# One pool of eight PSUM banks, corrected durations and a new order for a planned recurrence-and-attention kernel

## The chip, the cores and the metric

One core of one Trainium2 chip. The metric is the device time of one execution in microseconds: 377.94 us, the median of three runs (376.17 to 379.87). The profiled execution took 377.4 us, of which the span from the first to the last instruction is 375.6 us.

## What is computed

Two stages, for batch 4, 768 positions, 8 heads of width 48 (model width 384). The first is a linear recurrence per head, the second an attention by four experts, two of which are kept per position.

```
for t in range(768):                      # per batch and head; state is 48 x 48
    y[t]  = r[t] @ (state + (u * k[t]) outer v[t])
    state = w[t][:, None] * state + k[t] outer v[t]
x = y, heads side by side                 # 4 x 768 x 384
for e in range(4):                        # q, k, v = x @ wq[e], x @ wk[e], x @ wv[e], width 64
    ye = softmax(causal(q k^T / 8)) v @ wo[e]
    out += (e among the top 2 of x @ w_gate) * gate weight * ye
```

All inputs and the output are float32.

## The kernel before

**Units.** The work is cut into eight units (batch b, half g of the sequence, 384 positions each). A unit has a recurrence part, `rwkv`, and an attention part, `moe`.

The recurrence part treats four pairs of heads, one after the other. A pair loads three tiles (`lt`, `nat`, `vy`). VectorE runs two scans over the decays (`suf` L376, `pre` L380); GpSimd or VectorE multiply keys and queries by them (`kt` L385, `mr` L387). TensorE transposes the scaled keys (`ktp` L415), which are copied to SBUF (`kts`). Three TensorE products follow: `aps` (L431, 24 matmuls of 64x64), masked by VectorE into `am`; `ups` (L445 and L446, 24 matmuls), copied into `ust` and scanned by VectorE into the states `ys` (L453); and `yps` (L475 and L478, 48 matmuls), which reads `am` and `ys` and is added to `xn` by VectorE (L484). After the pairs three transposes `xp` (L498) turn `xn` into `xh` and a rest `xl`, so that later products keep float32 accuracy in three passes.

The attention part projects `xh`, `xl` to queries and keys (`pp` L544) and to values and gate logits (`vp` L567). Then for two pairs of experts and three row blocks come scores (`sp` L632), maximum with mask on VectorE (L638), exponential on ScalarE (L644), transposes of the probabilities (`tp` L657) with their copies, the product with the values (`yp` L680), the gate weights (`gp`, `gb`), and the output projection (`op` L751) with its store.

**Tilings.** TensorE's array is used in four tilings, which the planner calls modes: the whole 128x128 (transposes, projections, `vp`, `op`, `gp`, `gb`, and the filler `warm`), 64x64 for `aps`, `ups`, `yps` (mode "q"), 64x128 for `sp` ("r"), 128x64 for `yp` ("h").

**What sets the order.** Nothing is scheduled by the compiler. `Plan.add` collects every step with a set of engines and their assumed durations, its data dependencies, its buffers, and a wished place in the order: `want`, the progress of its unit (from `T0`, `MV`, `LEAD`) plus an offset by kind (`OFF`, and `OFF0` for the first unit's recurrence). `Plan.order` then simulates all engines and emits the instructions engine by engine. At each step it takes, of those of an engine's first 40 candidates that could start within `SLACK` nanoseconds of the earliest, the one with the lowest `want`; on TensorE a candidate in the tiling that the array already has counts as lower by `STAY`. A change of tiling is charged `DRAIN` (100 ns) plus `ENTER` by kind. A step that needs a buffer is no candidate until one of its tag is free. Once emitted, the order on each engine is fixed; semaphores make it correct whatever the true durations are.

**PSUM.** There are eight banks. `bank(tag, ...)` takes one from the pool of its tag: four for `sc` (scores, always two at a time; one is held by the filler `warm` until its last matmul), two for `mo` (the attention's other products: `pp`, `vp`, `tp`, `yp`, `gp`, `gb`, `op`), two for `rw` (the recurrence: `ktp` 1, `aps` 1, `ups` 2, `yps` 2, `xp` 1). In the last unit `mo` products alternate between `mo` and `rw`. The table `BANK` can send a tag to another pool; it is empty.

**Fillers.** 94 matmuls `warm` on constant data keep TensorE busy: 14 at the start, 80 with the lowest urgency, which go where nothing else can start.

Of the kernel before, what the change touches and what calls it, by code (L numbers as in the profile page):

```python
# [41 lines left out]


def t_exp(cols):
    return 237 + 0.834 * cols


def t_pool(cols):
# [3 lines left out]
class Slot:  # L52
# [6 lines left out]
    def __call__(self):  # L59
        if self.ap is None:  # L60
# [6 lines left out]

WAITS = {"PE": dict(PE=0, DVE=215, ACT=215, POOL=260, SP=200), "DVE": dict(PE=139 + SAFE, DVE=127, ACT=128, POOL=164, SP=130),
         "ACT": dict(PE=164 + SAFE, DVE=143, ACT=127, POOL=170, SP=130), "POOL": dict(PE=150 + SAFE, DVE=140, ACT=150, POOL=128, SP=130),
         "SP": dict(PE=2000, DVE=2000, ACT=2000, POOL=2000, SP=2000)}  # L70

# [137 lines left out]
def rwkv_moe(ctx: ExitStack, tc: tile.TileContext, wkr, vY, nat, uN,  # L209
# [6 lines left out]
    plan = Plan()  # L216
    E_ = {"DVE": nc.vector, "ACT": nc.scalar, "POOL": nc.gpsimd, "SP": nc.sync}

    def sb(shape, dt, tag, name):
        return Slot(wk, shape, dt, tag, name)  # L220

    def bank(tag, name, dt=F32, whole=True):
        return Slot(ps, [128, 2048 // mybir.dt.size(dt)], dt, BANK.get(tag, tag), name, whole)

# [289 lines left out]
    def moe(b, g, v0, v1):  # L514
        xh, xl = XS[b, g]
# [59 lines left out]
        def gates():  # L575

            m1 = sb([128, 3], F32, "m1", f"m1{n0}")
            rank = sb([128, 3, E], F32, "rank", f"rank{n0}")
            c1 = sb([128, 3, E, E], F32, "c1", f"c1{n0}")
            c2 = sb([128, 3, E, E], F32, "c2", f"c2{n0}")  # L580
            lgk = [(lg, i) for i in range(3)]

            V = nc.gpsimd

            def compare(e):
                la = lg()[:, :, None, :].to_broadcast([128, 3, E, E])
# [12 lines left out]
            plan.add("gate", {"POOL": 1440}, ranks, lgk + ["masks", m1], [c1, c2, rank, ge])  # L599
            plan.add("gate", {"ACT": 250}, lambda e: nc.scalar.activation(ge(), ge(), AF.Exp), [ge], [ge])  # L600
            plan.add("gate", {"DVE": 100}, lambda e: nc.vector.scalar_tensor_tensor(
                ge(), rank(), 1.5, ge(), op0=ALU.is_lt, op1=ALU.mult), [rank, ge], [ge])

            def norm(e):
                V.tensor_tensor(c1()[:, :, 0, 0:2], ge()[:, :, 0:2], ge()[:, :, 2:4], op=ALU.add)
                V.tensor_tensor(gs(), c1()[:, :, 0, 0], c1()[:, :, 0, 1], op=ALU.add)
                V.tensor_scalar(gs(), gs(), 1e-9, None, op0=ALU.add)
            plan.add("gate", {"POOL": 875}, norm, [ge, c1], [gs, c1])
# [79 lines left out]
        gg = sb([128, 3, E], F32, "gg", f"gg{n0}")  # L688
        gT = sb([128, 128], BF16, "gT", f"gT{n0}")

        def gather():

            g3 = sb([128, 128], BF16, "g3", f"g3{n0}")
            gp = mbank(f"gp{n0}", BF16)

            def over(e):
                nc.vector.scalar_tensor_tensor(gg(), asum(), 1e-9, gs()[:, :, None].to_broadcast([128, 3, E]),
                                               op0=ALU.add, op1=ALU.mult)
                nc.vector.reciprocal(gg(), gg())
# [12 lines left out]
            plan.add("g4", {"POOL": 1290}, parts, [gg], [gg, g3])  # L712
            plan.add("gp", {"PE": 60}, lambda e: nc.tensor.transpose(
                gp()[:, 0:128], g3(), identb), [g3], [gp])
            plan.add("gT", {"DVE": 131}, lambda e: nc.vector.tensor_copy(gT(), gp()[:, 0:128]), [gp], [gT])
# [42 lines left out]
        yps = []  # L758
# [15 lines left out]
        parts = [weigh(ep, yps[ep]) for ep in range(2)]  # L774
# [28 lines left out]
    for k, u in enumerate(units):  # L803
        spare[0] = k == len(units) - 1
        moe(*u, starts[k], starts[k] + MV[u[1]])
    for o in plan.order(dict(PE=7200.0 - 216 * WARM[0], DVE=3000.0, ACT=1700.0, POOL=3000.0, SP=560.0), SLACK):
        o["fn"](o["e"])


FLEX, LATE, SLACK = (True, True, 118.4)  # L810
BUFS = dict(lt=4, nat=3, ys=2, vy=3, suf=2, pre=3, am=2, kt=2, rk=2, kts=2, xn=2, xh=2, xl=2, lg=2, asum=2, ge=2, m1=2, rank=2, c1=1, c2=1,
            gs=2, mx0=6, mx1=4, a=4, gg=2, gT=2, g3=2, yr=2, yh0=1, yh1=1, yl0=1, yl1=1, ob=2, v_sb0=1, v_sb1=1, ATa=3, ATb=2,
            sc=4, mo=2, rw=2)
BUFS.update({f"{n}{l}{ep}": m for n, m in (("K", 1), ("Q", 2)) for l in "hl" for ep in range(2)})
# [78 lines left out]
```

## Time and profile before

| | |
|---|---|
| median of three runs | 377.94 us |
| the profiled execution | 377.4 us |
| its span | 375.6 us |
| TensorE matmul | 363.2 us, 97% |
| TensorE weight load | 281.4 us, 75% |
| VectorE | 309.2 us, 82% |
| ScalarE | 236.9 us, 63% |
| GpSimd | 144.3 us, 38% |
| granted TensorE clock, mean | 0.994 |

The busy time of an engine is the union of its instructions' durations. Matmuls are pipelined: one lasts longer than the distance to the next. So the time that a matmul costs is read from the start of one to the start of the next in the timeline, and a matmul that starts late shows no idle time while the one before it still counts as running.

### The profile page before, as it was taken

What the parts mean: (1) busy time and instruction counts of PE and PEld (TensorE: products, weight loads), DVE (VectorE), ACT (ScalarE), POOL (GpSimd) and SP (SyncE); (2) the same over time, 40 slices, a digit from 0 to 9 for tenths busy, and PEclk for the clock granted to TensorE, in tenths of its full rate; (3) what the DMA queues carried; (4) which work ended last, traced back from release to release, by engine and by line L of the source; (5) the groups of instructions that cost most, each with busy time, mean ns of one, the idle gap of its engine ahead of it and who ended that gap; (6) DMA issues with size and microseconds to landing.
All of it is one profiled execution on the core that took longest, in us unless ns stands there. A gap on an engine that the chain in (4) does not pass through costs nothing.

```text
span 375.6 us, 12545 instructions
## 1 busy us (share of the span) xinstructions
PE 363.2 (97%) x5046; PEld 281.4 (75%) x5046; DVE 309.2 (82%) x838; ACT 236.9 (63%) x658; POOL 144.3 (38%) x254
## 2 busy tenths in 40 slices
PE   6999999999999999999989999999999999999985
PEld 2555787778867778888876878888886878789653
DVE  6999999999997996999986996999996864467461
ACT  2475465975957767575765766575785754666562
POOL 3246666585651653263331553363431402002000
PEclk9899999999999999999999999999999999999999
DMA  7798454544543444525324343624222001001001
GB/s 231 282 353 268 144 172 132 184 130 137 189 138 128 128 128 122 185 78 191 112 83 126 112 145 92 193 83 135 75 65 65 3 3 65 1 2 63 2 2 65
DMA packets 18059, 45.18 MB, mean 120 GB/s; under 512 B 2000, under 2 KB 9424, under 8 KB 18000
## 3 DMA queue, kind: packets, MB, share of 16 engines
q1 hardware_dynamic: 18000, 44.37, 36.9%
q8 instruction: 40, 0.66, 0.7%
q14 instruction: 19, 0.16, 0.1%
HBM read 39.64 MB, written 4.72 MB: 118 GB/s over the span
## 4 chain that ended last, share of the span: by engine, by line
PE 80%; DVE 11%; DMA 3%; ACT 2%; issue 2%; POOL 1%; SPq 0%; POOLq 0%; DVEq 0%; ACTq 0%
PE pp L544 11%; PE yp L680 10%; PE sp L632 10%; PE tp L657 9%; PE vp L567 7%; PE op L751 6%; PE aps L431 5%; PE yps L475 5%; PE warm L791 4%; PE ups L445 3%; DVE suf L376 2%; PE ktp L415 2%; PE xp L498 2%; PE yps L478 2%; DVE ys L453 2%
## 5 line engine op out<-in xcount | busy, mean ns | idle before, releaser
L644 ACT ACTIVATE a<-a,mx 128x128 f32<-128x128 f32 (+5 forms) x96 | 63.8, 666 | 10.2 <-DVE mx L638 9.5
L657 PE MATMUL tp<-ident,a 128*128 128x128 f32 x336 | 56.6, 284 | 1.6 <-ACT a L644 1.0
L638 DVE CUSTOM_DVE_ANT_0 a<-sp,cmask 128x384 f32<-128x384 f32 (+4 forms) x96 | 44.8, 495 | 14.9 <-PE sp L632 14.2
L657 PEld LDWEIGHTS tp<-ident,a 128*128 128x128 f32 x336 | 37.3, 140 | 12.1 <-ACT a L644 5.5
L392 POOL TENSOR_TENSOR nat<-nat,u_sb 128x288 f32<-128x288 f32 x30 | 29.4, 979 | 37.9 <-PE tp L657 16.7
L227 ACT COPY ATa<-tp 128x512 f32<-128x512 f32 (+3 forms) x68 | 32.8, 487 | 16.5 <-PE tp L657 16.1
L385 POOL TENSOR_TENSOR kt<-lt,suf 128x384 f32<-128x384 f32 x27 | 29.2, 1082 | 23.5 <-DVE suf L376 16.3
L544 PE MATMUL pp<-xh,wh_qk 128*128 128x384 f32 x96 | 38.0, 396 | 0.0
L387 POOL TENSOR_TENSOR pre<-lt,pre 128x384 f32<-128x384 f32 x22 | 22.9, 1040 | 37.5 <-DVE pre L380 21.7
L405 ACT ACTIVATE xn<-nat,rk 128x48 f32<-128x48 f32 x117 | 30.0, 325 | 10.5 <-DVE rk L398 10.0
L680 PE MATMUL yp<-ATa,v_sb 128*64 128x384 f32 (+2 forms) x224 | 36.4, 450 | 0.0
L376 DVE TENSOR_TENSOR_SCAN suf<-lt,one_suf 128x390 f32<-128x390 f32 x32 | 34.3, 1078 | 2.3 <-DMA lt<-in_wkr_dram 2.0
L453 DVE TENSOR_TENSOR_SCAN ys<-ust,wdec 112x384 f32<-112x384 f32 x32 | 33.4, 1046 | 0.9 <-ACT ust L227 0.6
L380 DVE TENSOR_TENSOR_SCAN pre<-lt,inv_pre 128x390 f32<-128x390 f32 x32 | 32.6, 1018 | 0.1
L544 PE MATMUL pp<-xl,wh_qk 128*128 128x384 f32 x96 | 32.3, 337 | 0.0
L544 PE MATMUL pp<-xh,wl_qk 128*128 128x384 f32 x96 | 32.3, 336 | 0.0
L475 PE MATMUL yps<-ys,pre 64*64 64x48 f32 (+1 forms) x768 | 30.9, 262 | 0.1
L383 ACT COPY wdec<-suf 128x288 f32<-128x288 f32 x32 | 22.7, 710 | 12.9 <-DVE suf L376 6.7
L431 PEld LDWEIGHTS aps<-pre,kt 64*64 64x64 f32 x768 | 24.8, 134 | 7.5 <-issue 3.1
L791 PE MATMUL warm<-one_suf 128*128 128x512 bf16 x94 | 28.3, 420 | 1.4 <-POOL one_suf L247 1.4
L431 PE MATMUL aps<-pre,kt 64*64 64x64 f32 x768 | 28.8, 222 | 0.4
L475 PEld LDWEIGHTS yps<-ys,pre 64*64 64x64 f32 (+1 forms) x768 | 21.6, 133 | 9.0 <-issue 2.5
(135 smaller groups left out, 944.3 us busy)
## 6 DMA issues: line engine op xcount, KB each, us to landing
lt<-in_wkr_dram SPq DMA_DIRECT2D x31, 579.5 KB, 4.1
nat<-in_nat_dram SPq DMA_DIRECT2D x32, 432.0 KB, 3.4
vy<-in_vY_dram SPq DMA_DIRECT2D x32, 144.0 KB, 2.2
out_dram<-ob SPq DMA_DIRECT2D x24, 192.0 KB, 1.9
w_qk<-in_wqk_dram SPq DMA_DIRECT2D x1, 768.0 KB, 5.7
w_vg<-in_wvg_dram SPq DMA_DIRECT2D x1, 390.0 KB, 6.2
lt<-in_wkr_dram SPq DMA_DIRECT2D x1, 384.0 KB, 5.1
w_o<-in_wo_dram SPq DMA_DIRECT2D x1, 384.0 KB, 6.7
```

What stands on the lines that cost most here:

```text
L227: nc.scalar.copy(o, i)
L376: plan.add("suf", {"DVE": t_scan(WB)}, lambda e, suf=suf, w_=w_: nc.vector.tensor_tensor_scan(rev(suf()), rev(w_()), rev(one_suf), 0.0, op ...
L431: nc.tensor.matmul(a_[half(h), c * C:(c + 1) * C], k[half(h), c, :], m[half(h), c, 0:C], start=True, stop=True)
L453: plan.add("ys", {"DVE": t_scan(D * NX)}, lambda e, ys=ys, us=us, wd=wd: nc.vector.tensor_tensor_scan(flat(ys()[0:112]), flat(us[0:112]), ...
L475: nc.tensor.matmul(yps[h]()[half(q), o], pre()[r, c, 0:C], ys()[r, :, c], start=i == 0, stop=False)
L544: nc.tensor.matmul(pp()[:, 0:384], w[:, qk, k, cs], x()[:, k, :], start=(k == j == 0), stop=(k == j == 2))
L632: nc.tensor.matmul(sps[x]()[:, 0:w], q()[p, t], flat(k())[p, o], start=j == 0, stop=j == 2)
L638: plan.add("max", {"DVE": t_dve(w) + T_RED}, lambda e, x=x, a=a, mx=mx, h=h, o=o, m=m, sps=sps: nc.vector.tensor_tensor_reduce(a()[:, o], ...
L644: plan.add("exp", {"ACT": t_exp(n)}, lambda e, x=x, y=y, mx=mx, a=a: nc.scalar.activation(a()[:, 0:n], a()[:, 0:n], AF.Exp, bias=mx[-1](), ...
L657: nc.tensor.transpose(tp()[:, j * 128:(j + 1) * 128], a()[:, (j0 + j) * 128:(j0 + j + 1) * 128], ident)
L680: nc.tensor.matmul(yp()[e * 64:e * 64 + 64, lo:384], v_sb[ep]()[:, j, e * 64:e * 64 + 64], at, start=(j == 0), stop=(j == nj - 1))
L791: plan.add("warm", {"PE": 216}, lambda e: nc.tensor.matmul(w()[:, 0:512], wz[:, 0:128], wz, start=True, stop=True), [], [w], want=1e6 if i ...
```

## The change

The instructions, their data and their shapes stay. Three things change. First, `BANK` sends the tags `rw` and `sc` to `mo`, whose pool now has all eight banks, so any product may take any free bank. Second, the planner's assumptions: an exponential costs 40 ns more, a maximum 12 ns more, the GpSimd steps `gate` (L599) and `g4` (L712) 190 and 1160 ns more; a load counts as landed 2700 ns after its issue instead of 2000, and small loads cost 200 ns more; VectorE is free at 3800 ns instead of 3000, the load queue at 740 instead of 560. Third, the order is another: every offset in `OFF` and `OFF0`, the pacing `MV`, `LEAD`, `T0`, `T1`, the `SLACK`, and `STAY`, which goes from 3.04 to 12.46.

```diff
 def t_exp(cols):
-    return 237 + 0.834 * cols
+    return 277 + 0.834 * cols
...
-         "SP": dict(PE=2000, DVE=2000, ACT=2000, POOL=2000, SP=2000)}
+         "SP": dict(PE=2700, DVE=2700, ACT=2700, POOL=2700, SP=2000)}
...
-        plan.add(kind, {"SP": max(475.0 if cols > 0 else 650.0, abs(cols) * 512 / 360.0)},
+        plan.add(kind, {"SP": max(475.0 if cols > 0 else 650.0, abs(cols) * 512 / 390.0 + (200.0 if abs(cols) < 400 else 0.0))},
...
-            plan.add("gate", {"POOL": 1440}, ranks, lgk + ["masks", m1], [c1, c2, rank, ge])
+            plan.add("gate", {"POOL": 1630}, ranks, lgk + ["masks", m1], [c1, c2, rank, ge])
...
-            plan.add("g4", {"POOL": 1290}, parts, [gg], [gg, g3])
+            plan.add("g4", {"POOL": 2450}, parts, [gg], [gg, g3])
...
-    for o in plan.order(dict(PE=7200.0 - 216 * WARM[0], DVE=3000.0, ACT=1700.0, POOL=3000.0, SP=560.0), SLACK):
+    for o in plan.order(dict(PE=7200.0 - 216 * WARM[0], DVE=3800.0, ACT=1700.0, POOL=3000.0, SP=740.0), SLACK):
         o["fn"](o["e"])
...
-FLEX, LATE, SLACK = (True, True, 118.4)
+FLEX, LATE, SLACK = (True, True, 126.8)
...
-            sc=4, mo=2, rw=2)
+            mo=8)
...
-BANK = {}
+BANK = {'rw': 'mo', 'sc': 'mo'}
...
-T_RED = 0
+T_RED = 12
...
-MV = {0: 29.57, 1: 45.97}
-LEAD = (-8.87, -3.98)
+MV = {0: 25.79, 1: 54.18}
+LEAD = (-2.91, -8.85)
...
-STAY = 3.04
+STAY = 12.46
...
-T0, T1 = (30.81, 25.29)
+T0, T1 = (28.53, 22.07)
```

## Rows read from the trace of the kernel before

**Rows 1.** The page's first two parts: busy time of each engine with its share of the span, and the granted TensorE clock in 40 equal slices (tenths of full speed).

```profile
PE 363.2 (97%) x5046; PEld 281.4 (75%) x5046; DVE 309.2 (82%) x838; ACT 236.9 (63%) x658; POOL 144.3 (38%) x254
...
PEclk9899999999999999999999999999999999999999
```

**Rows 2.** The view by stretches: from and to in us, length, then busy us and number of instructions of PE, PEld, DVE, ACT and POOL, the granted clock, the DMA share and GB/s.

```profile
0.00:40.00 40.00, 35.80 (x514) 20.51 (x515) 34.90 (x74) 18.73 (x48) 18.86 (x30) 0.96 0.81 281
40.00:362.00 322.00, 318.05 (x4480) 255.21 (x4479) 270.83 (x757) 214.50 (x604) 124.62 (x221) 1.00 0.33 104
137.60:223.36 85.76, 83.97 (x1240) 67.81 (x1239) 75.28 (x207) 56.84 (x158) 34.14 (x60) 1.00 0.41 127
```

**Rows 3.** The timeline of TensorE (start, length, line, operation, tiles, number merged): the first and the last stay in a tiling between 40 and 362 us, and the two places where the same stretch of one batch begins anew.

```profile
40.57 0.91 PE L431 MATMUL aps<-pre,kt 64*64 64x64 f32 x24
...
137.60 0.88 PE L498 MATMUL xp<-ident,xn 128*128 128x128 f32 x6
...
223.36 0.87 PE L498 MATMUL xp<-ident,xn 128*128 128x128 f32 x6
...
362.65 2.03 PE L680 MATMUL yp<-ATa,v_sb 128*64 128x384 f32 x8
```

**Rows 4.** The same timeline at places that show the price of a change of tiling: one projection step alone between two `ups`, one `aps` alone, and two `aps` on end, each with what starts next.

```profile
42.96 0.44 PE L544 MATMUL pp<-xh,wh_qk 128*128 128x384 f32 x1
43.24 0.33 PE L544 MATMUL pp<-xh,wl_qk 128*128 128x384 f32 x1
43.41 0.34 PE L544 MATMUL pp<-xl,wh_qk 128*128 128x384 f32 x1
43.71 0.25 PE L445 MATMUL ups<-nat,kts 64*64 64x48 f32 x1
...
163.95 0.91 PE L431 MATMUL aps<-pre,kt 64*64 64x64 f32 x24
164.79 0.44 PE L544 MATMUL pp<-xh,wh_qk 128*128 128x384 f32 x1
...
168.25 1.61 PE L431 MATMUL aps<-pre,kt 64*64 64x64 f32 x48
169.80 0.34 PE L724 MATMUL gb<-gT,sel 128*128 128x128 bf16 x3
```

**Rows 5.** The view of single lines: all TensorE instructions of a line with their number, duration in ns (least, median, most), and first and last start.

```profile
L431 PE MATMUL aps<-pre,kt x768: 217/218/268, 12.9 to 317.2; 64*64 64x64 f32 x192
...
L445 PE MATMUL ups<-nat,kts x384: 218/218/339, 11.0 to 315.7; 64*64 64x48 f32 x192
...
L475 PE MATMUL yps<-ys,pre x768: 244/266/279, 14.9 to 318.8; 64*64 64x48 f32 x183, 48*64 48x48 f32 x9
...
L632 PE MATMUL sp<-Kh,Qh x128: 301/409/502, 53.1 to 357.7; 64*128 64x384 f32 x48, 64*128 64x320 f32 x32, 64*128 64x128 f32 x16, 64*128 64x256 f32 x16
```

**Rows 6.** Who waited for whom (us in total, times, longest): all that TensorE's matmuls waited for by 0.7 us or more.

```profile
PE ktp L415 <- DVE inv_pre L378: 2.8, 2, 2.3
PE warm L791 <- POOL one_suf L247: 1.4, 1, 1.4
PE xp L498 <- DVE xn L484: 1.0, 1, 1.0
PE tp L657 <- ACT a L644: 1.0, 2, 0.7
PE ktp L415 <- POOL g L708: 0.7, 2, 0.4
```

**Rows 7.** The timeline at the start and the end of the work: the first and the seventh scan `suf`, the first projection, the last product of the recurrence, the last matmul.

```profile
7.24 0.97 DVE L376 TENSOR_TENSOR_SCAN suf<-lt,one_suf 128x390 f32<-128x390 f32 x1 [2.01 <-DMA lt<-in_wkr_dram]
...
35.62 0.96 DVE L376 TENSOR_TENSOR_SCAN suf<-lt,one_suf 128x390 f32<-128x390 f32 x1
...
41.45 0.53 PE L544 MATMUL pp<-xh,wh_qk 128*128 128x384 f32 x1
...
318.78 0.36 PE L478 MATMUL yps<-vy,am 64*64 64x48 f32 x5
...
371.54 0.34 PE L751 MATMUL op<-wh_o,yl 128*128 128x384 f32 x1
```

**Rows 8.** What the planner's new durations can be held against: the exponential and the maximum (columns: number, busy us, mean ns, idle before), one instance of the gate split on GpSimd, first and last instruction, and the loads' time to landing (page, part 6).

```profile
L644 ACT ACTIVATE a<-a,mx 128x128 f32<-128x128 f32 (+5 forms) x96 | 63.8, 666 | 10.2 <-DVE mx L638 9.5
L638 DVE CUSTOM_DVE_ANT_0 a<-sp,cmask 128x384 f32<-128x384 f32 (+4 forms) x96 | 44.8, 495 | 14.9 <-PE sp L632 14.2
...
164.24 0.79 POOL L708 CAST g<-gg 128x12 bf16<-128x12 f32 x1 [0.52 <-DVE gg L700]
...
165.66 0.21 POOL L711 TENSOR_TENSOR g<-gg,g 128x12 bf16<-128x12 f32 x1
...
lt<-in_wkr_dram SPq DMA_DIRECT2D x31, 579.5 KB, 4.1
```

**Rows 9.** The timeline of TensorE at two score steps of 384 columns on end, with what starts next.

```profile
344.25 0.44 PE L632 MATMUL sp<-Kh,Qh 64*128 64x384 f32 x2
...
345.49 0.33 PE L657 MATMUL tp<-ident,a 128*128 128x128 f32 x1
```

**Rows 10.** The clock: stretches as in rows 2, one in the start-up and one that holds the 22 transposes in a row, and these in the timeline.

```profile
10.00:13.00 3.00, 3.00 (x34) 1.30 (x34) 2.37 (x5) 1.38 (x4) 0.92 (x2) 0.59 1.03 420
...
358.60:362.80 4.20, 3.35 (x23) 2.48 (x24) 3.65 (x14) 3.83 (x10) 0.00 (x0) 1.00 0.01 2
...
358.68 1.58 PE L657 MATMUL tp<-ident,a 128*128 128x128 f32 x10 [0.28 <-ACT a L644]
360.93 1.79 PE L657 MATMUL tp<-ident,a 128*128 128x128 f32 x12 [0.68 <-ACT a L644]
```

More of the change, by code (lines that the diff above doesn't have):

```diff
@@ L812 @@
             gs=2, mx0=6, mx1=4, a=4, gg=2, gT=2, g3=2, yr=2, yh0=1, yh1=1, yl0=1, yl1=1, ob=2, v_sb0=1, v_sb1=1, ATa=3, ATb=2,
-            sc=4, mo=2, rw=2)
+            mo=8)
 BUFS.update({f"{n}{l}{ep}": m for n, m in (("K", 1), ("Q", 2)) for l in "hl" for ep in range(2)})
-BANK = {}
-OFF = {'ld': -12.27, 'ldn': 10.32, 'ldv': -96.62, 'wload': -30.38, 'wsplit': -87.24, 'masks': 1.11, 'ldu': 152.8, 'uk': 60.94, 'ur': 1.49, 'rk': 16.33, 'ux': 34.51, 'ktp': 2.24, 'kts': -8.09, 'aps': 3.79, 'am': -23.68, 'ups': -2.83, 'us': -78.16, 'ys': -70.57, 'carry': -20.34, 'yps': -40.48, 'addy': -115.55, 'mr': 4.5, 'suf': -4.8, 'st': 117.22, 'yl': 25.98, 'wd': 59.62, 'xh': -31.11, 'yh': -16.2, 'ql': -17.17, 'ev': 9.05, 'pre': 3.38, 'g3': 30.08, 'warm': 79.99, 'ob': 53.53, 'lg': -12.14, 'sc': -0.66, 'yr': -122.15, 'xp': -6.34, 'gate': 2.24, 'inv': 6.41, 'gT': -33.58, 'y': -31.87, 'v': -98.59, 'exp': 23.75, 'op': -1.5, 'qd': 12.96, 'xl': 0.4, 'gp': -79.67, 'kt': 49.38, 'gb': -119.18, 'tp': 5.13, 'proj': -0.22, 'av': 6.36, 'vproj': 0.89, 'max': 12.4, 'g4': -42.26}
+BANK = {'rw': 'mo', 'sc': 'mo'}
@@ new lines @@
+OFF = {'ld': 22.89, 'ldn': -30.77, 'ldv': -83.63, 'wload': 15.02, 'wsplit': -248.33, 'masks': -40.37, 'ldu': 54.71, 'uk': 47.97, 'ur': 51.09, 'rk': 107.52, 'ux': 28.97, 'ktp': -4.2, 'kts': -69.37, 'aps': -11.54, 'am': 2.27, 'ups': 3.16, 'us': -47.67, 'ys': -83.96, 'carry': -18.84, 'yps': 0.53, 'addy': -98.48, 'mr': -1.74, 'suf': 44.37, 'st': 132.26, 'yl': 66.9, 'wd': 107.04, 'xh': -0.12, 'yh': 17.28, 'ql': -92.45, 'ev': 93.99, 'pre': 20.56, 'g3': 74.68, 'warm': 296.26, 'ob': 149.07, 'lg': 94.26, 'sc': -4.35, 'yr': -252.37, 'xp': 9.52, 'gate': 9.43, 'inv': -28.67, 'gT': -176.06, 'y': -38.04, 'v': -236.23, 'exp': 62.69, 'op': -27.47, 'qd': -56.89, 'xl': -7.03, 'gp': -35.65, 'kt': 32.08, 'gb': -208.95, 'tp': 3.8, 'proj': -0.16, 'av': -2.05, 'vproj': 6.31, 'max': 16.74, 'g4': 55.63}
@@ L819 @@
 T_SC = {128: 180, 256: 345, 384: 505, 512: 670, 320: 432}
-T_RED = 0
+T_RED = 12
 ENTER = dict(proj=105, vproj=105, op=105, tp=56, ktp=56, xp=56, gb=40, sc=120, aps=50, yps=10, av=10)
 MU = {0: 5.9 + 3 + 3.84 + 4.1 + 2.9, 1: 5.9 + 3 + 9.6 + 8 + 2.9}
-MV = {0: 29.57, 1: 45.97}
-LEAD = (-8.87, -3.98)
+MV = {0: 25.79, 1: 54.18}
+LEAD = (-2.91, -8.85)
 WARM = (14, 80)
 UXA = True
-STAY = 3.04
-OFF0 = {'ld': -109.52, 'ldv': -183.4, 'ldn': -107.92, 'ldu': -160.76, 'wload': -69.8, 'masks': 37.99, 'wsplit': 35.5, 'suf': -22.08, 'pre': -42.91, 'us': 102.15, 'rk': 24.01, 'ql': -55.84, 'proj': 2.04, 'kt': -33.03, 'xl': -15.64, 'aps': -23.82, 'qd': -40.23, 'vproj': -68.79, 'ur': -32.53, 'kts': 19.21, 'yh': -112.49, 'gate': -74.16, 'gb': 77.05, 'carry': -41.65, 'ys': -69.04, 'inv': 80.31, 'am': -40.1, 'ktp': 73.73, 'yl': 1.14, 'xh': -14.61, 'y': -64.95, 'op': -24.98, 'av': 12.7, 'warm': -2.53, 'mr': -86.44, 'st': 99.04, 'gT': -10.75, 'lg': 20.16, 'yps': -53.3, 'sc': -93.55, 'uk': 4.31, 'gp': -67.29, 'ux': -6.81, 'ev': 95.26, 'max': -120.86, 'tp': -29.71, 'xp': -107.46, 'wd': -112.92, 'g3': 50.7, 'ups': -31.57, 'exp': -134.77, 'yr': 131.09, 'ob': -69.84, 'v': 48.22, 'addy': -40.22, 'g4': 26.0}
-T0, T1 = (30.81, 25.29)
+STAY = 12.46
+OFF0 = {'ld': -190.63, 'ldv': -246.33, 'ldn': -91.82, 'ldu': -155.02, 'wload': -54.04, 'masks': -118.8, 'wsplit': 12.52, 'suf': -49.48, 'pre': -63.78, 'us': 203.26, 'rk': 75.97, 'ql': -40.23, 'proj': -14.9, 'kt': 10.48, 'xl': -63.34, 'aps': -105.26, 'qd': -107.78, 'vproj': 112.78, 'ur': -0.87, 'kts': -42.75, 'yh': -86.96, 'gate': 44.79, 'gb': 170.29, 'carry': -15.82, 'ys': -108.1, 'inv': 42.19, 'am': -19.21, 'ktp': 77.38, 'yl': 31.29, 'xh': -40.81, 'y': -91.36, 'op': 25.46, 'av': -30.52, 'warm': 19.52, 'mr': -78.87, 'st': 145.01, 'gT': 29.27, 'lg': 34.34, 'yps': -27.04, 'sc': -80.04, 'uk': 58.99, 'gp': -113.55, 'ux': -1.98, 'ev': 81.11, 'max': -20.68, 'tp': -9.38, 'xp': -199.74, 'wd': -49.53, 'g3': 43.84, 'ups': -5.75, 'exp': -9.84, 'yr': 38.65, 'ob': 14.86, 'v': 59.64, 'addy': -35.71, 'g4': -84.72}
+T0, T1 = (28.53, 22.07)
 NWD = 2
```

## The prediction

> **What bounds the kernel now.** I read the busy shares first: TensorE 97%, VectorE 82%, ScalarE 63% [rows 1]. Then the stretches, because these shares are means. Until 40 us VectorE is busy for 34.9 us [rows 2], and the first projection starts at 41.45 us [rows 7]: this is the start-up, one unit's recurrence through VectorE, and TensorE is fed with fillers. From 40 to 362 us TensorE is busy for 318.05 of 322 us, VectorE for 270.83 (84%) [rows 2]. After that a short chain ends the kernel. The list of waits has little for TensorE: 2.8 + 1.4 + 1.0 + 1.0 + 0.7 = 6.9 us, over half of it in the start-up [rows 6]. So between 40 and 362 us nothing is gained by ending waits; TensorE must do less, or lose less between its instructions.
>
> What it loses is found in the timeline. The order repeats: the same six `xp` begin a stretch at 137.60 and again at 223.36, so one batch takes 85.76 us [rows 3], with VectorE busy for 75.28 of them, 88% [rows 2]. I counted the stays in one tiling along it: 64 in a batch (24 in the whole array, 23 with 64x64, 12 with 64x128, 5 with 128x64), and 240 from 40 to 362 us, from the first to the last of [rows 3]. A change of tiling has a price. One `aps` takes 0.84 us to the next start, two on end 1.55 us: parting them costs 2 x 0.84 - 1.55 = 0.13 us on the 64x64 side. A projection step of three matmuls between two `ups` takes 43.71 - 42.96 = 0.75 us; at its inner distance of 0.17 us three would take 0.51, so 0.24 more on the side of the whole array, some of which stays when another kind of whole-array work stands before it [rows 4]. A stay taken out of a run thus removes two changes for 0.13 to 0.37 us, 0.07 to 0.18 each; I take **0.15 us a change**, near the upper end, because most stays removed would have a run of projections or transposes on the other side. In a batch that is 64 x 0.15 = 9.6 us, and none of it shows as idle time.
>
> That busy time hides this is also what the Trainium skill says (Perfetto Trace Analysis, Identifying the Most-Contended Engine): matmul busy share is no good measure of how near the limit TensorE is, the share of the weight loads is better. By busy share only 375.6 - 363.2 = 12.4 us would be open, by the weight loads 375.6 - 281.4 = 94.2 us; my sum needs neither, and the distances between starts lie between the two.
>
> **Banks: why a batch has 23 short stays with 64x64.** Lines 431, 445/446 and 475/478 have 768, 2 x 384 and 2 x 768 matmuls [rows 5]; at 24, 24 and 48 a step these are 32 steps each, 24 steps in a batch. 24 steps in 23 stays means that they practically never stand together. The pool explains it: `rw` has two banks, `aps` takes one, `ups` and `yps` two each. Only `aps` beside `aps` fits, and the one doubled stay is just that, the x48 in [rows 4]. Of eight common banks any two of these steps take at most four, so they fit together, and of the other four the filler holds one until its last matmul and the first expert pair's `yp` one. The ready work must still be there: the three steps of one pair hang on each other through copies and a scan, but those of neighbouring pairs don't, and `STAY` at 12.46 lets TensorE reach that much further ahead for them.
>
> **The sum.**
> - Tiling changes. I expect two recurrence steps to a stay on average: 24 steps in 12 stays, 11 fewer. Scores 12 to 10, since two probabilities' buffers of four are taken by each step and `sp` can't run far ahead of `tp`. Of the whole-array stays some 6 vanish, as their neighbours join; the 128x64 stays remain. 64 - 19 = 45 in a batch. 19 x 0.15 = 2.85 us a batch; 322 / 85.76 = 3.75 batches: **-10.7 us**. Ends: none fewer, 0; and triples throughout (8 + 8 + 4 + 12 = 32 stays), 32 x 0.15 x 3.75 = -18 us. No other work hides this, since TensorE is without idle time here; VectorE would go from 88% to 75.28 / 82.9 = 91%.
> - Start-up. The 32 or so stays before 41 us cost nothing: VectorE sets that time, 34.9 of 40 us [rows 2]. The first scan starts when its load lands, at 7.24 us, and that stays; a better order can move work for later units out of the way. Seven `suf` scans stand from 7.24 to 35.62 us [rows 7], and the first unit needs four: three of about 1 us are another's. Ends 0 and -3 us; I take **-1 us**.
> - Durations. The exponential's mean of 666 ns, the loads' 4.1 us and the 1.6 us from 164.24 to 165.87 for the split [rows 8] say that the old figures for loads and split were short, the new split figure of 2.45 us rather long. What an instruction late by them can cost now is in the waits, 0.7 us on `g` and 1.0 on `a` [rows 6]. Ends 0 and -2 us; **-0.5 us**.
> - Longer runs of one kind fill the banks faster than they are emptied. The trace before has no such runs, so bounds: 0, and the second rival's 20 us below; nearest are the waits of 1.0 us on `a`. I take **+1.5 us**.
> - The new order of SP's loads and stores and of GpSimd's steps: the DMA engines are busy for 33% of the stretch, GpSimd for 34.14 us of a batch [rows 2], and TensorE waits for no load [rows 6], so I cost both at nothing; if a load or a GpSimd product came late, VectorE or `aps` would wait, and VectorE's 9% to spare would cover some 7 us a batch.
>
> Together -10.7 us: 377.4 - 10.7 = 366.7 us for an execution like the profiled one; the median of the runs stands 0.5 us above it, so **367 us**. This likeliest case spans 360 to 372 us.
>
> **The rivals.**
> - *Nothing gained, 376 us.* A stay decides only among steps that are ready within `SLACK`, 127 ns. If copies, masks and scans, not banks, are what keeps the recurrence steps apart, TensorE has nothing to stay for, and the change doesn't do what it says. For it: a pair's three steps are a chain, and VectorE is at 88%. Against: the only pair of steps that the banks allowed did join. 377.4 - 1 - 0.5, between 373 and 379.
> - *More gained, 357 us.* The 32 stays, -18 us, and -3 in the start-up, +1: 349 to 360. Against it, VectorE would stand at 75.28 / 81 = 93%.
> - *Slower, 383 us: runs bound by their evacuation.* Its place is a run of scores. Two score steps of 384 columns take TensorE 1.24 us [rows 9], the four maxima that empty their banks 4 x 495 = 1.98 us [rows 8], so TensorE gains 0.37 us a step on VectorE until the banks are full, and thereafter waits 0.37 us, and longer where VectorE has a scan of 0.97 us [rows 7] in between, some 0.6 us. Before, scores stood in ones and twos with other work between. There are 64 score steps (128 first-pass matmuls, two a step [rows 5]). It decides from about 24 of them waiting (24 x 0.6 = 14.4 us, which eats the 10.7 and makes 1% more); with 27 and the lost joins: 366.7 + 16 = 383. Against: four probability buffers stop such a run after two steps.
> - *The clock, 383 us.* Longer stays gather transposes too. The granted clock, 0.59 in a stretch of the start-up (part at 1.2, part at 2.4 GHz), was 1.00 through the longest run of them, 22 in 4.2 us with two gaps [rows 10]. If a run of this length fell to half clock it would cost about 2 us; two in each of four batches, 16 us. The Trainium skill (TensorE: Matmul & The Clock Gate, Part 4) says that transposes don't count as activity for the clock, which would make such a fall likely; the trace speaks against it, for the clock's digit is 9 in every slice after the second [rows 1].
>
> **How the numbers follow.** Chances: forecast 0.55, more 0.13, nothing 0.16, evacuation 0.13, clock 0.03. From no change one can tell about 1%, 3.8 us. Faster: 0.55 + 0.13 = 0.68; same 0.16; slower 0.13 + 0.03 = 0.16. The range 356 to 380 takes in the likeliest case, the nothing case and the upper half of the larger gain; it leaves out about 0.07 below and 0.12 above.
>
> **What would show it.** Stays between 40 us and the tail: about 170 instead of 240, with `aps`, `ups`, `yps` in runs of 48 matmuls and more; a batch of about 83 us; VectorE at 90% or more in it; first projection at 40 us; clock 1.00. Stays as many as before would show that banks weren't what parted them. Fewer stays with the same time would show that the price returned as waits on `sp` or `tp` evacuations, which the list of waits of TensorE and its weight loads would name; a last `yps` well after 318.78 us [rows 7] would show that the recurrence, not TensorE, had become late.

## The result and the profile after

The changed kernel takes **360.31 us** (median of four runs, 359.93 to 360.86) against 377.36 us (376.17 to 379.87) for the kernel before on the same chip: a ratio of 0.954, 95% interval 0.949 to 0.959, or 17 us less. The forecast was 367 us; the measured time lies in the range (356 to 380), at the lower end of the likeliest case's own range of 360 to 372.

The profiled execution took 359.95 us, with a span of 358.2. Its busy shares and granted clock, to be held against [rows 1]:

```profile
PE 341.6 (95%) x5046; PEld 279.8 (78%) x5046; DVE 309.0 (86%) x847; ACT 232.0 (65%) x653; POOL 138.8 (39%) x250
...
PEclk9969999999999999999999999999999999999999
```

The same 5046 matmuls keep TensorE busy 21.6 us less (363.2 to 341.6); the time without a matmul grew by 4.2 us (span less busy: 12.4 to 16.6). VectorE's work is as before, 309 us. All of the gain is TensorE's time between one instruction and the next.

**Where it was gained.** I cut both executions at the same places of the work: when the last transpose `xp` of the first, the third and the eighth unit starts (columns as in [rows 2]). The planner mixes units, so the number of matmuls in a stretch differs a little between the two. The kernel before:

```profile
0.00:39.90 39.90, 35.70 (x513) 20.41 (x514) 34.80 (x73) 18.64 (x47) 18.76 (x30) 0.96 0.81 281
39.90:109.60 69.70, 69.46 (x1117) 55.81 (x1116) 67.46 (x177) 48.78 (x145) 44.68 (x65) 1.00 0.51 155
109.60:320.40 210.80, 208.21 (x3068) 167.37 (x3066) 178.40 (x496) 138.51 (x387) 77.21 (x144) 1.00 0.33 104
320.40:375.60 55.20, 49.87 (x356) 37.80 (x353) 28.57 (x94) 30.98 (x80) 3.63 (x17) 0.99 0.06 23
```

The kernel after:

```profile
0.00:41.00 41.00, 33.89 (x483) 19.24 (x484) 32.57 (x68) 16.08 (x39) 15.84 (x28) 0.92 0.74 251
41.00:109.40 68.40, 66.11 (x1123) 57.00 (x1122) 67.37 (x175) 48.80 (x146) 38.17 (x59) 1.00 0.49 156
109.40:306.70 197.30, 196.15 (x3110) 168.78 (x3108) 179.40 (x508) 138.90 (x395) 80.31 (x144) 1.00 0.36 116
306.70:358.20 51.50, 45.46 (x338) 34.74 (x335) 29.67 (x100) 28.18 (x75) 4.44 (x21) 1.00 0.07 24
```

My count of the changes of tiling in the timeline stands beside it:

| stretch | before: us, changes | after: us, changes | gained |
|---|---|---|---|
| first unit | 39.9, 26 | 41.0, 18 | -1.1 us |
| units two and three | 69.7, 62 | 68.4, 32 | 1.3 us |
| units four to eight | 210.8, 160 | 197.3, 73 | 13.5 us |
| the rest | 55.2, 24 | 51.5, 17 | 3.7 us |
| all | 375.6, 272 | 358.2, 140 | 17.4 us |

Read the second and third line together. In units two and three 30 changes were saved for 1.3 us, because VectorE is busy for 67.46 of 69.70 us there, before, and for 67.37 of 68.40 after: hardly any of that time is left to gain on TensorE, and most of what TensorE saved turned into time without a matmul, 2.3 us of it (69.70 - 69.46 became 68.40 - 66.11). From there on VectorE had room (178.40 of 210.80 us, 85%), and 87 changes saved go with 13.5 us, 0.155 us each if nothing else made the gain there. In the rest, 15 projection matmuls fewer were left over (36 `pp` against 51), at 0.17 us 2.6 of its 3.7 us. Over the whole kernel 132 changes went with 17.4 us, 0.13 each.

**What the runs look like.** The timeline of TensorE after (start, length, line, tiles, number merged), at the two places where the stretch of one batch begins anew:

```profile
151.84 0.54 PE L680 MATMUL yp<-ATa,v_sb 128*64 128x384 f32 x2
...
230.10 0.54 PE L680 MATMUL yp<-ATa,v_sb 128*64 128x384 f32 x2
```

A batch takes 78.26 us, before 85.76 [rows 3], with 28 stays in one tiling instead of 64: 9 in the whole array, 9 with 64x64, 6 with 64x128, 4 with 128x64 (before 24, 23, 12, 5). VectorE is busy for 73.89 us of it, 94%:

```profile
151.84:230.10 78.26, 77.41 (x1240) 67.13 (x1239) 73.89 (x208) 57.45 (x168) 34.13 (x61) 1.00 0.43 140
```

One stay with 64x64, and one of scores, in the same batch:

```profile
162.41 0.39 PE L475 MATMUL yps<-ys,pre 64*64 64x48 f32 x8
...
163.28 0.81 PE L431 MATMUL aps<-pre,kt 64*64 64x64 f32 x21
...
164.27 0.22 PE L445 MATMUL ups<-nat,kts 64*64 64x48 f32 x1
164.43 0.23 PE L713 MATMUL gp<-identb,g 128*128 128x128 bf16 x1
...
168.64 0.50 PE L632 MATMUL sp<-Kh,Qh 64*128 64x512 f32 x2
169.44 0.31 PE L632 MATMUL sp<-Kh,Qh 64*128 64x320 f32 x2
169.88 0.31 PE L632 MATMUL sp<-Kh,Qh 64*128 64x320 f32 x2
170.32 0.34 PE L632 MATMUL sp<-Kh,Qh 64*128 64x384 f32 x2
171.12 0.44 PE L415 MATMUL ktp<-ident,kt 128*128 128x128 f32 x2
```

A whole `yps`, `aps` and `ups` stand in one stay, and four score steps on end: four steps of two banks are all eight banks.

**The waits after**, TensorE's and VectorE's largest (us in total, times, longest), against [rows 6]:

```profile
PE yps L475 <- issue: 2.3, 1, 2.3
PE ups L445 <- DMA nat<-in_nat_dram: 1.5, 1, 1.5
...
PE tp L657 <- ACT a L644: 1.1, 2, 0.6
```

```profile
DVE a L638 <- PE sp L632: 6.5, 7, 3.2
```

The two largest of TensorE lie in the start-up. None of TensorE's matmuls waits for a maximum, the step that empties the banks of the scores. Its weight loads do, for 3.6 us in all, 0.5 at the longest, against 2.3 and 0.6 before. VectorE's idle time before the maxima fell from 14.2 us [rows 8] to 6.5; long runs of scores may feed it better, but that wasn't tried.

### The profile page after: what moved, and what is told of

It is laid out like the page before. It is cut to its first block, busy times and chain, and to the rows that moved or that the text cites. A ratio compares the mean times of both kernels' runs of the same rounds, so it can differ in the third digit from the quotient of the medians.

```text
span 358.2 us, 12575 instructions
## 1 busy us (share of the span) xinstructions
PE 341.6 (95%) x5046; PEld 279.8 (78%) x5046; DVE 309.0 (86%) x847; ACT 232.0 (65%) x653; POOL 138.8 (39%) x250
## 4 chain that ended last, share of the span: by engine, by line
PE 65%; DVE 22%; ACT 4%; issue 4%; DMA 3%; SPq 1%; DVEq 0%; ACTq 0%
PE pp L544 11%; PE yp L680 8%; PE tp L657 8%; PE op L751 7%; PE vp L567 6%; PE sp L632 6%; PE aps L431 4%; PE yps L475 4%; DVE ys L453 4%; DVE a L638 3%; DMA nat<-in_nat_dram 3%; DVE pre L380 3%; PE warm L791 2%; PE yps L478 2%; PE ktp L415 2%
## 5 line engine op out<-in xcount | busy, mean ns | idle before, releaser
L657 PE MATMUL tp<-ident,a 128*128 128x128 f32 x336 | 48.8, 277 | 1.3 <-ACT a L644 1.1
L385 POOL TENSOR_TENSOR kt<-lt,suf 128x384 f32<-128x384 f32 x27 | 30.4, 1127 | 42.1 <-DVE suf L376 21.1
L227 ACT COPY ATa<-tp 128x512 f32<-128x512 f32 (+3 forms) x76 | 34.6, 491 | 5.1 <-PE tp L657 5.0
L544 PE MATMUL pp<-xh,wh_qk 128*128 128x384 f32 x96 | 37.0, 386 | 0.1
L475 PE MATMUL yps<-ys,pre 48*64 48x48 f32 (+1 forms) x768 | 31.2, 263 | 3.7 <-issue 2.3
L453 DVE TENSOR_TENSOR_SCAN ys<-ust,wdec 112x384 f32<-112x384 f32 x32 | 32.3, 1028 | 1.7 <-ACT ust L227 1.7
L383 ACT COPY wdec<-suf 128x288 f32<-128x288 f32 x32 | 23.0, 726 | 14.2 <-DVE suf L376 12.6
L376 DVE TENSOR_TENSOR_SCAN suf<-lt,one_suf 128x390 f32<-128x390 f32 x32 | 30.0, 956 | 0.7 <-DMA lt<-in_wkr_dram 0.7
L478 PE MATMUL yps<-vy,am 64*64 64x48 f32 x768 | 28.6, 223 | 0.1
L478 PEld LDWEIGHTS yps<-vy,am 64*64 64x64 f32 x768 | 26.0, 154 | 2.8 <-issue 2.5
L387 POOL TENSOR_TENSOR pre<-lt,pre 128x384 f32<-128x384 f32 x16 | 17.6, 1100 | 27.2 <-DVE pre L380 10.9
```

What stands on the lines that cost most here:

```text
L227: nc.scalar.copy(o, i)
L385: plan.add("kt", prod(384), lambda e, k_=k_, sfv=sfv, kt=kt: E_[e].tensor_tensor(kt(), k_(), sfv()[:, :, 1:C + 1], op=ALU.mult), [(lt, 1), ...
L453: plan.add("ys", {"DVE": t_scan(D * NX)}, lambda e, ys=ys, us=us, wd=wd: nc.vector.tensor_tensor_scan(flat(ys()[0:112]), flat(us[0:112]), ...
L475: nc.tensor.matmul(yps[h]()[half(q), o], pre()[r, c, 0:C], ys()[r, :, c], start=i == 0, stop=False)
L478: nc.tensor.matmul(yps[h]()[half(q), o], am()[half(h), c, :], vy()[half(h), c, :], start=False, stop=i == 2)
L544: nc.tensor.matmul(pp()[:, 0:384], w[:, qk, k, cs], x()[:, k, :], start=(k == j == 0), stop=(k == j == 2))
```

## The experiments

Twelve kernels, each timed beside the kernel before. The changes are counted in the order as it is written out; "idle" is the span less TensorE's busy time. The traces of e1 to e4 and e7 to e9 lack 6 to 15 of the 94 fillers `warm`; at 0.22 us from one filler to the next, their idle times may be too long by 1.3 to 3.3 us (an estimate), and their busy times too short.

| kernel | us | ratio to before | changes | TensorE busy | idle |
|---|---|---|---|---|---|
| before | 377.4 to 378.8 | 1 | 272 | 363.2 | 12.4 |
| e1 pool alone | 369.28 | 0.974 (0.970 to 0.978) | 220 | 350.1 | 17.4 |
| e2 `STAY` alone | 387.73 | 1.023 (1.020 to 1.027) | 271 | 365.8 | 21.2 |
| e3 pool and `STAY` | 372.12 | 0.983 (0.980 to 0.985) | 170 | 348.6 | 21.5 |
| e9 pool and durations | 366.18 | 0.970 (0.965 to 0.975) | 211 | 351.1 | 13.1 |
| e6 pool, `STAY`, durations | 360.31 | 0.952 (0.950 to 0.954) | 161 | 343.6 | 14.5 |
| after | 360.31 | 0.954 (0.949 to 0.959) | 140 | 341.6 | 16.6 |
| e4 after, banks split | 403.74 | 1.066 (1.063 to 1.070) | 242 | 370.8 | 30.7 |
| e5 after, short `STAY` | 371.77 | 0.982 (0.979 to 0.986) | 213 | 353.8 | 15.0 |
| e8 after, old durations | 363.74 | 0.964 (0.959 to 0.969) | 164 | 346.5 | 15.8 |
| e7 after, loads reordered | 360.97 | 0.956 (0.952 to 0.961) | 140 | 341.4 | 18.9 |
| p1 after, 80 small products | 385.08 | 1.017 (1.014 to 1.019) | 275 | 368.6 | 15.0 |
| p2 after, 80 whole products | 371.77 | 0.982 (0.979 to 0.985) | 140 | 355.5 | 14.3 |
| e10 after, old start-up, other offsets again | 355.36 | 0.939 (0.936 to 0.943) | 135 | 341.7 | 13.2 |

**The pool alone** (e1), in the kernel before:

```diff
-            sc=4, mo=2, rw=2)
+            mo=8)
-BANK = {}
+BANK = {'rw': 'mo', 'sc': 'mo'}
```

> The kernel before with the eight banks as one pool and nothing else; offsets, durations and the stay of 3.04 are the old ones. Counted in its TensorE order there are 220 changes of tiling instead of 272. Banks first (my theory: the split into four, two and two kept steps of one tiling apart, and a change costs 0.15 to 0.21 us): 52 x 0.15 to 0.21 = 8 to 11 us less, 366 to 370 us. Order first (rival: the offsets and the pacing made the gain, the pool alone is of little use): within 1% of 377 us.

52 changes fewer, 8.8 us less than the 378.12 us of the kernel before beside it: 0.17 us a change, with the old offsets, the old `STAY` and the old durations. Counted in the two traces, the stays with 64x64 fell from 94 to 71 and those of scores from 49 to 28; before, no run of scores had more than two steps, here 12 have three or four. The banks did keep the steps apart.

**The longer stay alone** (e2), in the kernel before:

```diff
-STAY = 3.04
+STAY = 12.46
```

> The kernel before with the stay of 12.46 and nothing else. 271 changes of tiling instead of 272. Banks first: with two banks for the recurrence there is nothing to stay for, 374 to 381 us. Stay first (rival: the longer stay alone makes the gain): 372 us or less.

One change fewer, and 9.6 us more: outside what either theory said. That a longer stay finds nothing to join with two banks for the recurrence was right; that it then does no harm was wrong. Of the 11.4 us between the two profiled spans (387.0 and 375.6), 6.9 lie in units two and three, cut as above (76.6 us against 69.7, busy 73.0 against 69.5). The granted clock was at half there for a while:

```profile
103.90:107.20 3.30, 3.30 (x21) 2.53 (x21) 2.64 (x9) 1.15 (x4) 0.92 (x1) 0.50 0.47 105
```

The 8.8 us more of idle time in the table are in part the 15 missing records.

**Both** (e3): the two diffs above together.

> The kernel before with the common pool and the stay of 12.46, old offsets and durations. 170 changes of tiling. Banks first: 102 x 0.15 to 0.21 = 15 to 21 us less than before, 356 to 362 us, most of the whole change's gain of 17 us. Order first: over 370 us.

A miss for theory one. The time lies in the rival's range, over 370 us, but e6 below has the same offsets and takes 360. The changes went to 170, yet the time is 2.8 us above that of the pool alone. TensorE's waits show part of the reason:

```profile
PE tp L657 <- ACT a L644: 3.4, 3, 2.4
PE yps L475 <- DVE ys L453: 2.8, 5, 0.9
PE ktp L415 <- DVE inv_pre L378: 2.5, 1, 2.5
```

The probabilities and the scanned states came later than the order assumed; the idle time is 4.1 us above that of e1. But 50 changes fewer should also have saved busy time, and it fell by 1.5 us only. One part of that is the clock: after the wait of 2.4 us for `a` it was at half for 3.4 us, and 12 transposes took 2.81 us, where the last 12 of the changed kernel take 1.79:

```profile
354.36 2.81 PE L657 MATMUL tp<-ident,a 128*128 128x128 f32 x12 [2.36 <-ACT a L644]
```

```profile
354.40:357.80 3.40, 3.40 (x15) 2.95 (x16) 1.59 (x5) 1.78 (x4) 0.76 (x4) 0.50 0.01 2
```

What took the rest is open.

**The banks split again in the changed kernel** (e4):

```diff
-            mo=8)
+            sc=4, mo=2, rw=2)
-BANK = {'rw': 'mo', 'sc': 'mo'}
+BANK = {}
```

> The changed kernel with the banks split into four, two and two again; offsets, durations and the stay of 12.46 are the new ones. 242 changes of tiling instead of 140. Banks first: 102 x 0.15 to 0.21 = 15 to 21 us more than 360, so 375 to 381 us, and more where the new order waits for banks that are not there. Order first: 366 us or less.

Slower than theory one's 375 to 381 us, which it had left open upwards: 403.74 us. The 242 changes are 102 more than after, at 0.155 us 15.8 us; the time is 43 us longer. Of the rest, idle time is up to 14.1 us (30.7 against 16.6), and part may be the clock, granted at 5 and 6 tenths in two slices; what that cost isn't parted from the rest:

```profile
PEclk9999569999999999999999999999999999999999
```

```profile
40.00:60.00 20.00, 17.02 (x235) 14.48 (x237) 15.53 (x33) 7.91 (x23) 7.42 (x8) 0.59 0.44 145
```

So the offsets chosen for eight common banks are no good for split ones, and this run can't be read as the price of the split alone.

**The short stay in the changed kernel** (e5):

```diff
-STAY = 12.46
+STAY = 3.04
```

> The changed kernel with the stay of 3.04. 213 changes of tiling instead of 140. If a change costs what I took, 0.15 us: 73 x 0.15 = 11 us more than 360, 371 us; if it costs 0.21 us, as the batch of the two traces says: 375 us. If the longer stay did nothing (rival: pool and offsets made the gain): 363 us or less.

73 changes more, 11.5 us more: 0.157 us each (by the two ratios, each to the kernel before beside it, 10.7 us, 0.15 each). With common banks, corrected durations and the new offsets, `STAY` is worth what it removes.

**The price by itself** (p1 and its control p2): in 80 places of the changed kernel a product of constants is added behind a group of `pp`, `vp` or `op`, into columns that nobody reads; in p1 with 64x64, in p2 in the whole array. The order of all else is that of the kernel after.

```diff
...
+                    if k == 2:
+                        nc.tensor.matmul(pp()[0:64, 448:496], one_suf[0:64, 0:64], one_suf[0:64, 0:48], start=True, stop=True)
...
```

> The changed kernel, its order unchanged, with one matmul of 64x64 by 48 columns more behind each of 32 query and key projections, 24 value projections and 24 output projections, into columns of the bank that nobody reads: 80 single visits to the tiling of 64x64 in runs of the whole array, 160 changes at most, fewer where the run ends there anyway. Against the control with the same number of whole-array matmuls, a price of 0.15 us gives 24 us more, 0.21 us gives 34 us more, 0.07 us (the lowest of my readings) 11 us; if changes cost nothing (rival: the gain came from evacuations that were no longer waited for), the two are the same within 2 us.

> The control: the same 80 places with a matmul of 128x128 by 48 columns, so no change of tiling is added. By any theory the time of the changed kernel plus 80 times the matmul and its weights, some 0.1 us each: 360 + 4 to 12 us.

p1 has 135 changes more than p2 and takes 13.3 us longer (385.08 - 371.77): **0.10 us a change**. That is less than the 0.15 taken and more than the lowest reading of 0.07. The two differ in the size of the weights too: a load in p1 takes 131 ns, in p2 188. One place in p1, where the product is two instructions of L547:

```profile
126.13 0.34 PE L544 MATMUL pp<-xl,wh_qk 128*128 128x384 f32 x1
126.40 0.31 PE L547 MATMUL pp<-one_suf 64*64 64x48 f32 x2
126.64 0.44 PE L544 MATMUL pp<-xh,wh_qk 128*128 128x384 f32 x1
```

and one in p2:

```profile
123.59 0.34 PE L544 MATMUL pp<-xl,wh_qk 128*128 128x384 f32 x1
123.77 0.31 PE L547 MATMUL pp<-one_suf 128*128 128x48 f32 x2
123.90 0.42 PE L544 MATMUL pp<-xh,wh_qk 128*128 128x384 f32 x1
```

From projection to projection 0.51 us against 0.31: 0.20 for two changes, in and out. The weight loads show what happens. In p1 the load engine has a gap ahead of each of the 80 small products' loads, in p2 it has none; p1's load at the same place:

```profile
125.96 0.19 PEld L544 LDWEIGHTS pp<-xl,wh_qk 128*128 128x128 f32 x1
126.40 0.19 PEld L547 LDWEIGHTS pp<-one_suf 64*64 64x64 f32 x2 [0.25 <-issue]
```

The load for the other tiling starts with its own matmul at 126.40, not beside the one before, so it is not hidden. That agrees with the Trainium skill (TensorEngine Tiling (Array Packing), Tiling Modes), which says that a change of mode drains TensorE. The page gives no time; the runs give 0.10 us.

**The old offsets** (e6): the changed kernel with `OFF`, `OFF0`, `MV`, `LEAD`, `SLACK`, `T0` and `T1` of the kernel before, which is the kernel before with pool, `STAY` and durations.

```diff
-T0, T1 = (28.53, 22.07)
+T0, T1 = (30.81, 25.29)
...
```

> The changed kernel with the old offsets, pacing and slack; pool, stay and durations are the new ones. 161 changes of tiling instead of 140. Banks and stay first: 21 x 0.15 to 0.21 = 3 to 4 us more than 360, 363 to 365 us. Order first (rival: the new offsets made the gain): over 370 us.

360.31 us, the time of the changed kernel itself and less than either theory said. The new offsets remove 21 changes, and the remainder after the last `xp` of the eighth unit is shorter with them (51.5 us against 64.3), but the first unit ends at 41.0 us instead of 35.4: by themselves they are worth nothing here.

**The old durations** (e8, in the changed kernel) **and the new ones with the pool alone** (e9, in the kernel before):

```diff
-    return 277 + 0.834 * cols
+    return 237 + 0.834 * cols
...
-T_RED = 12
+T_RED = 0
```

> The changed kernel with the planner's old durations; pool, stay and offsets are the new ones. 164 changes of tiling instead of 140. If only changes count: 24 x 0.15 = 4 us more than 360, 363 to 365 us. If the durations are what separates the kernel before with pool and stay (372 us at 170 changes) from the one with durations as well (360 us at 161): 368 to 374 us.

> The kernel before with the common pool and the new durations; stay and offsets are the old ones. 211 changes of tiling; with the pool alone it was 369 us at 220. If only changes count: 9 x 0.15 = 1 us less than that, 368 us. If the durations are worth the 12 us that lie between the kernels with pool and stay, without and with them: 357 to 361 us.

e8 takes 3.4 us more, with 24 changes more (24 x 0.155 = 3.7), as its first theory said; e9 falls between its two. Between e1 and e9 the durations are worth about 3 us (ratios 0.974 and 0.970, intervals that overlap), with 9 changes between them. Between e3 and e6 they are worth 12 us (372.12 and 360.31), with 9 changes: here they take away idle time (21.5 to 14.5 us, of which the 11 missing records of e3 may be 2.4) and 5 us of busy time. So in these runs the durations matter most where the stay is long and the offsets are not chosen for it. Which of the seven changed lines does it was not tried; the one for loads also has a rate of 390 in place of 360. And from e9 to e6 only `STAY` differs: 50 changes fewer and 5.9 us less, 0.12 each.

**The first loads in another order** (e7): the changed kernel, its first 15 loads issued with the tiles of the first pairs ahead of the weights.

```diff
...
+    first = [o for o in todo if o["e"] == "SP"][:15]
...
+    ahead += kinds["wload"]
+    for o in ahead + [o for o in todo if not any(o is x for x in ahead)]:
```

> The changed kernel with the first 15 loads issued in another order on their queue (first pair's decays, keys and its natural tile, then the other pairs one after the other, the weights last); the order on every other engine is the same. In the changed kernel the first state product waits for its natural tile until 15.15 us, a later one sits idle for 2.3 us, the clock is at half from 21.2 to 28.0 us, and the first unit's recurrence ends at 41.0 us against 35.4 with the old offsets. If the late loads are the cause and TensorE bounds everything behind: first unit done at 35 to 37 us, 354 to 357 us in all. If the start-up is covered by something behind it (VectorE, or the second unit's loads): 359 to 361 us.

No gain: the first unit ends at 40.6 us instead of 41.0, the time is the same. The wait of 1.5 us for `nat` is replaced by others of the start-up, 3.3 us of `aps` on `pre` and 2.4 of `ktp` on `kt`. The order of loads alone isn't what makes the new start-up late.

**The old start-up under the new order** (e10): the changed kernel with `OFF0`, `T0` and `T1` of the kernel before, and `OFF`, `MV`, `LEAD`, `SLACK` (111.7) and `STAY` (12.65) chosen again for it.

```diff
-STAY = 12.46
+STAY = 12.65
...
-T0, T1 = (28.53, 22.07)
+T0, T1 = (30.81, 25.29)
...
```

> The changed kernel (pool, stay and durations as they are) with the start-up's offsets and due times of the kernel before, and the other offsets chosen again for them: 135 changes of tiling instead of 140. Theory one: the changed kernel loses some 5 us in its start-up, since its first unit's gate and recurrence end at 41.0 us and those of the run with the old offsets at 35.4; that run had 21 changes more (21 x 0.16 = 3.4 us) and took the same time, so without them the gain of the start-up shows: first six xp done by 36 us and 354 to 357 us in all. Theory two: TensorE's total work sets the time whatever the first unit does, since it is fed with other work meanwhile; then only 5 changes are saved, under 1 us: 359 to 361 us.

**355.36 us** (six runs, 354.45 to 357.06): 5 us faster than the changed kernel, and the intervals of the two ratios are apart. This is the version that beats both. Cut as above:

```profile
0.00:39.30 39.30, 34.03 (x488) 19.48 (x489) 33.85 (x71) 17.73 (x46) 18.76 (x27) 0.96 0.76 262
39.30:110.00 70.70, 69.37 (x1190) 59.58 (x1189) 68.70 (x184) 48.68 (x145) 42.22 (x61) 1.00 0.52 162
110.00:303.40 193.40, 192.75 (x3038) 166.59 (x3036) 178.94 (x509) 134.00 (x394) 78.87 (x142) 1.00 0.35 115
303.40:354.90 51.50, 45.50 (x338) 34.72 (x335) 29.50 (x99) 27.98 (x74) 3.64 (x17) 1.00 0.07 24
```

TensorE is as busy as after (341.65 against 341.60), and the 3.3 us by which the spans differ are idle time. The time is theory one's, but its first mark failed: the first unit ends at 39.3 us, not by 36, after one wait of 2.9 us of `ktp` for `inv_pre`. Of the idle time 1.84 us less lie in the first unit (7.11 to 5.27), 0.96 in units two and three, 0.50 in units four to eight. So the larger part of the idle time saved lies in the first unit. Whether the old start-up gives it, or the offsets that were chosen anew beside it, this run doesn't show, for it changes both.

## Why the prediction was right and wrong

- **What bounds the kernel** was right: TensorE, by what it loses between instructions. The span fell by 17.4 us, more than the 12.4 us that its busy share had left open. That bears out the rule that the prediction cites (the Trainium skill, Perfetto Trace Analysis, Identifying the Most-Contended Engine): 97% busy did not mean 3% to gain.
- **The price**, 0.15 us a change, was right as what a change saved goes with where TensorE is the bound: 0.155 in units four to eight, 0.157 between e5 and after, 0.17 between before and e1, though 0.12 between e9 and e6, and from e1 to e3 50 changes fewer went with 2.8 us more. The bare change is 0.10. What makes up the other 0.05 wasn't measured by itself, so that 0.15 came out is in part luck.
- **The number of stays is the step that failed.** "24 steps in 12 stays" became 24 in 9, "12 to 10" for the scores became 16 steps in 6 stays, and of the whole array's stays 15 vanished where "some 6" were expected; 28 stays stood where the sum had 45. For the scores the reason was wrong: the probabilities' four buffers don't bound their runs, since such a buffer is taken by the maximum behind the scores and not by `sp`. The banks come nearer to it: most long runs have three or four steps. The sum's other end, "triples throughout", 32 stays, was nearer. But eight banks are no firm bound of four steps, for at 335.87 five stand on end, ten banks' worth, so banks had come free within the run:

```profile
335.87 0.51 PE L632 MATMUL sp<-Kh,Qh 64*128 64x512 f32 x2
...
338.09 0.58 PE L632 MATMUL sp<-Kh,Qh 64*128 64x384 f32 x2
```

- **Where the price counts** was wrong too, the other way. The sum took 3.75 batches, all of 40 to 362 us, and VectorE by its mean. In units two and three VectorE was at 97% already, and 30 changes gave 1.3 us there instead of 4.5. With the right count, 36 x 0.15 x 3.75 would have been 20 us; 17 were measured. The two errors pull opposite ways, so it is partly luck that 367 came within 7 us of the time.
- **Start-up**: -1 us was forecast, +1.1 measured, outside its ends of 0 and -3, and it stayed hidden behind the larger gain. The first projection came at 42.70 us, not at 40 (41.45 in [rows 7]). The stays before 41 us that the sum put at some 32 were 28.
- **Durations**: -0.5 us with ends 0 and -2 was too small. Undone in the changed kernel they cost 3.4 us, about what their 24 changes are worth. That fits with their acting through the order that they lead to more than through single late instructions, and the sum had no such term.
- **Longer runs**: +1.5 us. TensorE's waits on `a` stayed at 1.1 us, and its weight loads waited 1.3 us more for maxima than before (3.6 against 2.3). Whether that cost time isn't shown.
- **The rivals.** *Nothing gained* fell: banks were what parted the steps, as e1 shows alone. *More gained* is where the kernel went, by its own mechanism of triples (24 steps in 9 stays), short of its 357 us by the first 110 us. *Evacuation* did not come: TensorE ran four score steps on end, with VectorE at 94%; no matmul of its list waits on a maximum, and no weight load for over 0.5 us. What the prediction set against this rival, the four probability buffers, did not hold.
- *The clock* did not fall with transposes in the changed kernel. The longest run of them now has 30, where [rows 10] had 22:

```profile
338.95 1.09 PE L657 MATMUL tp<-ident,a 128*128 128x128 f32 x8
340.55 1.58 PE L657 MATMUL tp<-ident,a 128*128 128x128 f32 x10 [0.50 <-ACT a L644]
342.76 1.79 PE L657 MATMUL tp<-ident,a 128*128 128x128 f32 x12 [0.63 <-ACT a L644]
```

```profile
338.90:344.60 5.70, 4.48 (x32) 3.30 (x32) 5.63 (x22) 5.26 (x15) 0.01 (x1) 1.00 0.00 0
```

The clock is 1.00 through it. So the measurement decides against what the Trainium skill says (TensorE: Matmul & The Clock Gate, Part 4), that transposes don't count, as far as such a run goes. But the rival wasn't empty. In e3 (above) and in e9 the clock fell to half among the same last transposes, for 3.4 us each, after TensorE had waited there:

```profile
346.48 2.36 PE L657 MATMUL tp<-ident,a 128*128 128x128 f32 x10 [1.55 <-ACT a L644]
```

```profile
346.60:350.00 3.40, 3.08 (x14) 2.68 (x15) 1.24 (x4) 3.05 (x8) 0.00 (x0) 0.50 0.00 0
```

In e6 it waited as long, after 18 transposes and before 12 more, and the clock stayed at 1.00 (338 to 348 us):

```profile
343.25 1.79 PE L657 MATMUL tp<-ident,a 128*128 128x128 f32 x12 [1.57 <-ACT a L644]
```

What tells these cases apart is open.

- **The marks**: "about 170" stays from 40 us to the tail were 118 (before 240); the batch took 78.26 us, not 83; VectorE stood at 94% in it; the last `yps` came in the run below, 23 us before 318.78, and the last matmul at 353.62 us against 371.54 [rows 7], so the recurrence was not late.

```profile
296.14 0.25 PE L478 MATMUL yps<-vy,am 64*64 64x48 f32 x4
...
353.62 0.34 PE L751 MATMUL op<-wh_o,yl 128*128 128x384 f32 x1
```

## What to carry to other kernels

Where one engine works in several tilings or modes, count the stays along the timeline and price a change from places where the same work stands alone and in company; the busy share shows neither. To see how far runs can grow, ask for each step which buffer it claims itself and when, for those can limit it, and the buffers of later steps didn't here. And apply the price stretch by stretch: where another engine is at 97%, a change saved gives little (here 1.3 us for 30). A rule of an order (here `STAY`) can cost alone (+9.6 us) and with the buffers that let it work (+2.8 us on top of the pool), and pay once the durations are right too (-5.9 us with the old offsets, -11.5 with the new), so such parts don't add.

## What was not expected of the hardware

- In the start-up after, TensorE stops for 2.3 us in the middle of one product, with nothing to wait for in the profile:

```profile
22.22 0.25 PE L475 MATMUL yps<-ys,pre 48*64 48x48 f32 x1 [2.32 <-issue]
```

The instruction queue moved one packet of 16 KB then, which took 1.07 us. Stops of the same kind are in e5 (2.1 us), e7 (1.5), p1 (3.0) and p2 (3.0), which have this start-up. Among TensorE's waits of e6 and e10, which have the old one, and of e8, none of this kind is over 0.3 us. That late instructions are the cause is a guess; it wasn't tried.

- The granted clock was at half, 1.2 GHz, for 6.8 us from within that stop on:

```profile
21.20:28.00 6.80, 5.78 (x94) 3.63 (x97) 4.43 (x8) 2.95 (x8) 2.22 (x2) 0.50 0.47 141
```

The kernel before has a stretch at half in its start-up too, from 9.1 to 12.4 us, with TensorE busy throughout. In e6, with the old start-up, the clock is 0.999 over the whole run. The half clock of e4 lasted from 39.4 to 56.4 us; it began between two waits of TensorE, of 1.53 us up to 37.91 and of 1.18 us up to 40.61. Why it lasted 17 us, with TensorE busy for 13.45 of them, stays open.
